# A float64 weight conversion whose integer intermediate moves from SBUF to the shared PSUM banks

## The chip, the cores and the metric

The kernel runs on one core of a Trainium2 chip. The metric is the device time of one execution in microseconds (us), the median over several runs. Lower is better.

## The reference

Three layers follow each other. Attention comes first, with a bias that depends on the distance of two positions; then a dense layer, whose two weight matrices arrive as float64; then a layer of eight experts, of which each token uses two.

```python
scores = scale * np.matmul(q, k.transpose(0, 1, 3, 2))          # 2 x 8 heads, 576 positions, 64 wide
h = np.maximum(x @ w1 + b1, 0.0); bias = h @ w2                  # x: log-distance ratio, hidden size 32
attn = softmax(scores + bias.transpose(2, 0, 1)[None])
x = (attn @ v)                                                   # 1152 tokens x 512
h = x @ w_in; x = (h * (1.0 / (1.0 + np.exp(-h)))) @ w_out       # 512 x 2048 and 2048 x 512, float64
# experts: the two largest of eight noisy logits, softmax weights, relu(x @ w1[e]) @ w2[e]
```

## The kernel before, in words

All products are made in pairs of float16 numbers: a value is split into a high part `hi` and a rest `lo`, and TensorE multiplies hi by hi, hi by lo and lo by hi.

The positions are cut into five chunks a to e (ORDER). For each chunk there are three kinds of work. `bias_wave` (L324 on) makes the bias table: in each of its 18 steps VectorE writes a mask `mk` (L337), TensorE multiplies it 16 times into a PSUM tile `pb` (L345, L346), VectorE and ScalarE read `pb` (L359, L361), and GpSimd adds the two results (L117, the helper STT). `attention` makes, for each of eight heads and each of the two batch entries, the scores (`pq`, L388), adds the bias and takes the maximum (L431), the exponential (L436), the float16 split (`pr`: ScalarE L438, GpSimd L117, VectorE L442), a transpose by DMA and the product with v. `moe1` and `moe1b` make the dense layer: 16 steps of 12 matmuls into a PSUM tile `ph` (L553 to L555), a tanh by ScalarE (L557), a product by VectorE (L558), the split, and then the second product `py` (L576 to L578).

The change sits in `conv` (L486 to L515), which turns the float64 weights into float32 bits and splits them. It runs 32 times (two matrices, two halves each, eight pieces of 128 x 512 each). One piece is loaded by a DMA of ScalarE's queue into `raw` (L496). VectorE makes float32 bits out of its two 32-bit halves in three instructions, all writing one tile `tt` of int32: L500 takes the high word and shifts it, L504 puts the sign and top exponent bit in, L505 the top bits of the low word. L504 and L505 read `raw` and `tt` and write `tt` in place. ScalarE scales `tt` by 32 in place (L509) and writes `hi` (L510); GpSimd subtracts (L511) and writes `lo`. All pieces take this branch (CP has every index). `tt` uses the two slots of the tag "yT" in SBUF, so a slot is held from L500 to the end of L511.

PSUM has eight banks: two tiles of two banks under the tag "pq" (scores, accumulators), one bank "av", and three banks under the tag "gen", handed out by `gen()` (L147). `pb` of the bias waves, `ph` of the dense and the expert layer and a few smaller tiles take turns in these three. A bank goes to the next tile when every reader of the last one is done.

The order of the work is set in two places. `merge` (L672 on) interleaves the pieces of work in program order by PLAN, a hand-written table of a start and a step for each: here "ci" and "co" (the conversion), "aa" to "ad" (attention), "ba" to "be" (bias waves), "ma" to "md" and "na" (dense layer). The framework's scheduler then fixes one order of instructions for each engine from that priority and from a model of the times and of free slots, and puts in the semaphore waits. An engine runs its instructions in that order, so an instruction that waits holds up all behind it on the same engine.

Of the kernel before, what the change touches and what calls it, by code (L numbers as in the profile page):

```python
# [9 lines left out]
F32 = mybir.dt.float32  # L10
F16 = mybir.dt.float16
I32 = mybir.dt.int32
U32 = mybir.dt.uint32
AF = mybir.ActivationFunctionType
# [94 lines left out]
def body(ctx, tc, nc, A):  # L109
    out = A["out"]  # L110
    V, SC, G, PE, SP = nc.vector, nc.scalar, nc.gpsimd, nc.tensor, nc.sync
    mm = PE.matmul

    def STT(eng, o, x, scale, y, op=OP.subtract):

        if eng is G and scale == 1.0:
            G.tensor_tensor(o, x, y, op=op)  # L117
        else:
            V.scalar_tensor_tensor(o, x, scale, y, op0=OP.mult, op1=op)
# [6 lines left out]
    def follow(later, key):  # L126
        if key in LAST:
            after(later, LAST[key])
# [11 lines left out]
    ps = ctx.enter_context(tc.tile_pool(name="ps", bufs=1, space=PSUM))  # L140
    s_m1 = ExitStack()
    m1 = s_m1.enter_context(tc.tile_pool(name="m1", bufs=1, side="right"))
# [175 lines left out]
    def wtile():  # L318
        i = used[0] % 8
        used[0] += 1  # L320
        return WB[:, 4096 * i:4096 * i + 4096]
# [164 lines left out]
    def conv(key, half, src):  # L486

        hi, lo = wtile(), wtile()
        WT[key, half] = (hi, lo)
        for pc in range(8):  # L490
            if pc % 3 in RG.get((key, half), ()):
                raw = m1.tile([128, 512], mybir.dt.int64, name="raw", tag="gt", bufs=NGT)
            else:
                raw = m1.tile([128, 512], mybir.dt.int64, name="raw", tag="raw", bufs=NRAW)
            with tc.issue_after(LAST[GATE].ins):
                SC.dma_start(raw, src(pc))  # L496
            v = raw.bitcast(I32).rearrange("p (n t) -> p n t", t=2)
            lw, hw = v[:, :, 0], v[:, :, 1]
            tt = m1.tile([128, 512], I32, name="tt", tag="yT", bufs=2)
            i = V.tensor_scalar(tt, hw, 0x07FFFFFF, 3, op0=OP.bitwise_and, op1=OP.logical_shift_left)  # L500
            if (key, half) in GC:
                follow(i, GC[key, half])
            LAST["tt", key, half, pc] = i
            V.scalar_tensor_tensor(tt, hw, -1073741824, tt, op0=OP.bitwise_and, op1=OP.bitwise_or)  # L504
            V.scalar_tensor_tensor(tt, lw, 29, tt, op0=OP.logical_shift_right, op1=OP.bitwise_or)  # L505
            f = tt.bitcast(F32)
            cs = slice(512 * pc, 512 * pc + 512)
            if pc in CP[key][half]:
                SC.activation(f, f, AF.Copy, scale=32.0)  # L509
                SC.activation(hi[:, cs], f, AF.Copy)  # L510
                G.tensor_sub(lo[:, cs], f, hi[:, cs])  # L511
            else:
                SC.activation(hi[:, cs], f, AF.Copy, scale=32.0)
                STT(V, lo[:, cs], f, 32.0, hi[:, cs])
            yield  # L515

    def conv_in(half):
        w = A["w_in"].rearrange("(j p) f -> p j f", p=128)
        return conv("in", half, lambda pc: w[:, pc // 2, 1024 * half + 512 * (pc % 2):1024 * half + 512 * (pc % 2) + 512])

    def conv_out(half):
        w = A["w_out"].rearrange("(j p) d -> p j d", p=128)
        return conv("out", half, lambda pc: w[:, 8 * half + pc, :])
# [610 lines left out]
```

## Time and profile before

| what | us |
|---|---|
| median of 3 runs | 755.66 |
| lowest and highest of them | 752.59 and 762.42 |
| the profiled execution, its time | 758.37 |
| its span, first to last instruction | 756.6 |

The profile shows one execution. Engines are PE (TensorE), PEld (its weight loads), DVE (VectorE), ACT (ScalarE), POOL (GpSimd) and SP (the queue of most DMAs). A line such as L500 is a line of the kernel; L117 is the helper by which several places let GpSimd add or subtract. The duration of an instruction includes time in which it has started and cannot go on, so its shortest and its mean duration may differ.

### The profile page before, as it was taken

How to read it: one execution, taken by the hardware profiler on the slowest of the kernel's cores; microseconds unless marked ns; L12 is line 12 of the kernel's file. 1: busy time of each engine (PE TensorE's matmuls, PEld its weight loads, DVE VectorE, ACT ScalarE, POOL GpSimd, SP SyncE). 2: the span in 40 equal slices, each digit the busy share in tenths (PEclk: the TensorE clock that was granted, in tenths of full speed). 3: DMA queues.
4: the chain of work that ended last, by engine and by line, in shares of the span. 5: the costliest groups of instructions: out<-in, count | busy, mean ns of one | idle time of the engine just before them, and what ended most of it. 6: DMA issues, size and time to landing. Idle time of an engine off the chain costs nothing.

```text
span 756.6 us, 16562 instructions
## 1 busy us (share of the span) xinstructions
PE 606.9 (80%) x6371; PEld 402.6 (53%) x6371; DVE 502.3 (66%) x1093; ACT 377.9 (50%) x805; POOL 366.5 (48%) x366
## 2 busy tenths in 40 slices
PE   0565666578587878997999889979889899999992
PEld 0462344456344666565765664757665554655640
DVE  2999999999999699556952755656657642740200
ACT  2666467668644577345732644761355543541210
POOL 2686677687967687436761552303405114103022
PEclk9875557599788998998999999999999999999996
DMA  4547788778876699887996967764999959903123
GB/s 113 135 140 243 158 161 179 183 210 186 159 179 182 161 174 199 145 172 116 159 237 124 183 129 220 192 225 110 238 240 246 308 182 230 299 4 42 17 25 43
DMA packets 203143, 125.77 MB, mean 166 GB/s; under 512 B 153076, under 2 KB 175732, under 8 KB 203060
## 3 DMA queue, kind: packets, MB, share of 16 engines
q1 hardware_dynamic: 170868, 90.39, 52.2%
q10 hardware_dynamic: 27648, 24.32, 11.0%
q0 software_dynamic: 4544, 9.97, 7.1%
q8 instruction: 51, 0.84, 0.4%
q14 instruction: 32, 0.26, 0.1%
HBM read 74.83 MB, written 18.22 MB: 123 GB/s over the span
## 4 chain that ended last, share of the span: by engine, by line
PE 29%; DVE 29%; DMA 18%; issue 11%; ACT 4%; POOL 4%; SPq 3%; ACTq 1%; another core or an unknown queue 1%; DVEq 0%; POOLq 0%
DMA stg<-in_e 6%; DVE mk L337 4%; PE ph L979 3%; DVE z L431 3%; DMA pt<-pr 3%; PE ph L981 3%; DVE pr L442 3%; PE ph L980 3%; DVE tt L504 3%; DVE tt L505 3%; PE po L1010 3%; DVE tt L500 2%; PE po L996 2%; PE po L995 2%; PE po L997 2%
## 5 line engine op out<-in xcount | busy, mean ns | idle before, releaser
L117 POOL TENSOR_TENSOR pr<-z,pr 128x512 f16<-128x512 f32 x72 | 94.6, 1321 | 23.3 <-ACT pr L438 14.7
L553 PE MATMUL ph<-xT,wb 128*128 128x256 f16 (+1 forms) x320 | 84.9, 275 | 11.5 <-DVE th L558 7.1
L345 PE MATMUL pb<-rhs_h,mk 128*128 128x64 f16 (+1 forms) x720 | 66.4, 210 | 26.4 <-ACT ta L361 11.6
L337 DVE TENSOR_TENSOR mk<-io,tau 128x1024 f16<-128x1024 f16 (+1 forms) x90 | 85.8, 959 | 0.7 <-PE pb L346 0.7
L117 POOL TENSOR_TENSOR gt<-th,gt 128x256 f16<-128x256 f32 (+1 forms) x80 | 56.0, 704 | 60.6 <-ACT gt L562 58.1
L117 POOL TENSOR_TENSOR g<-ta 128x256 f32<-128x256 f32 (+1 forms) x72 | 63.6, 884 | 44.3 <-ACT ta L361 37.4
L554 PE MATMUL ph<-xT,wb 128*128 128x256 f16 (+1 forms) x320 | 84.8, 275 | 0.0
L555 PE MATMUL ph<-xT,wb 128*128 128x256 f16 (+1 forms) x320 | 84.8, 275 | 0.0
L958 POOL DMA_INDIRECT out<-ot,idx x18 | 27.6, 1536 | 114.5 <-ACT ot L964 52.5
L388 PE MATMUL pq<-km,qt 128*128 128x512 f16 (+2 forms) x160 | 51.7, 437 | 28.9 <-DVE st L431 28.4
L436 ACT ACTIVATE z<-z,st 128x576 f32<-128x576 f32 x72 | 55.3, 769 | 34.9 <-DVE st L435 34.4
L986 DVE SCALAR_TENSOR_TENSOR ht<-ph,ht 128x320 f16<-128x320 f32 (+2 forms) x80 | 32.8, 420 | 54.3 <-ACT ht L985 53.8
L345 PEld LDWEIGHTS <-mk 128*128 128x128 f16 (+1 forms) x720 | 57.8, 111 | 19.3 <-issue 7.7
L346 PEld LDWEIGHTS <-mk 128*128 128x128 f16 (+1 forms) x720 | 56.9, 112 | 20.1 <-issue 19.2
L346 PE MATMUL pb<-rhs_l,mk 128*128 128x64 f16 (+1 forms) x720 | 65.9, 209 | 0.0
L924 DVE SCALAR_TENSOR_TENSOR wb<-stg,wb 128x1024 f16<-128x1024 f32 (+1 forms) x48 | 48.3, 1042 | 23.6 <-ACT wb L923 20.2
L923 ACT ACTIVATE wb<-stg 128x1024 f16<-128x1024 f32 (+1 forms) x48 | 41.8, 908 | 33.5 <-DMA stg<-in_e 29.9
L576 PE MATMUL py<-wb,gt 128*128 128x512 f16 x144 | 56.0, 391 | 1.5 <-DVE st L431 1.3
L577 PE MATMUL py<-wb,gt 128*128 128x512 f16 x144 | 56.1, 389 | 1.1 <-POOL wb L511 1.1
L578 PE MATMUL py<-wb,gt 128*128 128x512 f16 x144 | 55.8, 388 | 0.0
L985 ACT ACTIVATE ht<-ph 128x320 f16<-128x320 f32 (+2 forms) x80 | 29.2, 378 | 50.0 <-PE ph L981 49.8
L511 POOL TENSOR_TENSOR wb<-tt,wb 128x512 f16<-128x512 f32 x32 | 43.7, 1366 | 17.3 <-ACT wb L510 17.1
(198 smaller groups left out, 1794.0 us busy)
## 6 DMA issues: line engine op xcount, KB each, us to landing
stg<-in_e SPq DMA_DIRECT2D x64, 512.0 KB
raw<-in_w_in ACTq DMA_DIRECT2D x16, 512.0 KB
raw<-in_w_out ACTq DMA_DIRECT2D x16, 512.0 KB
bt<-eb SPq DMA_DIRECT2D x24, 288.0 KB
eb<-g SPq DMA_DIRECT2D x12, 512.0 KB
yrows<-yh SPq DMA_DIRECT2D x9, 256.0 KB
out<-zero SPq DMA_DIRECT2D x3, 768.0 KB
bt<-eb SPq DMA_DIRECT2D x16, 144.0 KB
```

The costliest lines, as they stand in the source:

```text
L117: G.tensor_tensor(o, x, y, op=op)
L337: i = V.tensor_tensor(mk[:, :, :n], io16[:, None, i0:i0 + n].to_broadcast([128, 8, n]), tv, op=OP.is_gt)
L345: mm(pb[:n, :, t, :], m, rhs_h, start=True, stop=False)
L346: mm(pb[:n, :, t, :], m, rhs_l, start=False, stop=True)
L388: i = mm(pq[p0:p0 + n, :512].rearrange("p (m s) -> p m s", m=2), lt, KM[b][r0:r0 + nr, :, h].rearrange("p m x s -> p m (x s)"), start=star ...
L436: SC.activation(z, z, AF.Exp, bias=st[:, 2:3], scale=0.125, accum_out=sums[:, bi, h % 4:h % 4 + 1])
L553: mm(ph, hh[:, cs], xh, start=(j == 3), stop=False)
L554: mm(ph, hh[:, cs], xl, start=False, stop=False)
L555: mm(ph, hl[:, cs], xh, start=False, stop=(j == 0))
L576: mm(pys[i], gh, oh[:, cs], start=(f == 0), stop=False)
L577: mm(pys[i], gh, ol[:, cs], start=False, stop=False)
L578: mm(pys[i], gl, oh[:, cs], start=False, stop=(f == 15))
```

## The change

`tt` is taken from the "gen" banks of PSUM instead of the tag "yT" of SBUF. Since GpSimd works from SBUF here, ScalarE's first instruction no longer scales in place: it reads `tt` and writes a new float32 tile `fs` in SBUF, which takes the two "yT" slots, and the two instructions after it read `fs`. The number and the kind of instructions stay the same on every engine.

```diff
-            tt = m1.tile([128, 512], I32, name="tt", tag="yT", bufs=2)
+            tt = ps.tile([128, 512], I32, name="tt", tag="gen", bufs=3)
             i = V.tensor_scalar(tt, hw, 0x07FFFFFF, 3, op0=OP.bitwise_and, op1=OP.logical_shift_left)
...
             f = tt.bitcast(F32)
             cs = slice(512 * pc, 512 * pc + 512)
             if pc in CP[key][half]:
-                SC.activation(f, f, AF.Copy, scale=32.0)
-                SC.activation(hi[:, cs], f, AF.Copy)
-                G.tensor_sub(lo[:, cs], f, hi[:, cs])
+                fs = m1.tile([128, 512], F32, name="fs", tag="yT", bufs=2)
+                SC.activation(fs, f, AF.Copy, scale=32.0)
+                SC.activation(hi[:, cs], fs, AF.Copy)
+                G.tensor_sub(lo[:, cs], fs, hi[:, cs])
```

## Rows read from the trace of the kernel before

**Rows 1.** The page: busy time by engine, and VectorE's forty slices.

```profile
PE 606.9 (80%) x6371; PEld 402.6 (53%) x6371; DVE 502.3 (66%) x1093; ACT 377.9 (50%) x805; POOL 366.5 (48%) x366
...
DVE  2999999999999699556952755656657642740200
```

**Rows 2.** Busy time by stretch; last three columns: clock, DMA share, GB/s.

```profile
50.00:246.00 196.00, 130.25 (x1506) 86.34 (x1504) 194.59 (x340) 121.12 (x254) 146.70 (x125) 0.73 0.75 183
...
150.00:200.00 50.00, 37.83 (x444) 29.00 (x442) 49.11 (x100) 38.36 (x91) 41.27 (x38) 0.89 0.82 198
...
246.00:460.00 214.00, 187.62 (x2350) 133.34 (x2349) 140.59 (x387) 113.26 (x284) 123.60 (x148) 0.96 0.81 161
```

**Rows 3.** The chain that ended last, from 50 to 246 us, by line.

```profile
by line: issue 17.9%; DVE mk L337 12.4%; DVE tt L504 11.6%; DVE tt L505 9.9%; DVE tt L500 9.0%; DVE z L431 8.6%; DVE pr L442 8.0%; DVE ta L359 3.9%; DVE vl L119 2.6%; PE pq L388 2.4%; DVE sums L464 1.7%; POOL wb L511 1.6%; DVE xh L471 1.4%;
```

**Rows 4.** VectorE's groups by line from 50 to 246 us.

```profile
L337 DVE TENSOR_TENSOR mk<-io,tau 128x1024 f16<-128x1024 f16 x38 | 39.4, 1046 | 0.0
L505 DVE SCALAR_TENSOR_TENSOR tt<-raw,tt 128x512 int32<-128x512 int32 x32 | 34.8, 1086 | 0.3
L504 DVE SCALAR_TENSOR_TENSOR tt<-raw,tt 128x512 int32<-128x512 int32 x32 | 31.5, 983 | 0.3
L500 DVE TENSOR_SCALAR tt<-raw 128x512 int32<-128x512 int32 x32 | 22.8, 712 | 0.0
L442 DVE TENSOR_TENSOR pr<-z,pr 128x64 f16<-128x64 f32 x32 | 20.9, 659 | 0.0
...
L431 DVE CUSTOM_DVE_ANT_0 z<-pq,wb 128x576 f32<-128x576 f32 x16 | 11.9, 745 | 0.0
...
L558 DVE SCALAR_TENSOR_TENSOR th<-th,ph 128x256 f32<-128x256 f32 x16 | 6.4, 406 | 0.3 <-ACT th L557 0.3
```

**Rows 5.** The tile tt: shortest, median and longest duration, first and last start.

```profile
L500 DVE TENSOR_SCALAR tt<-raw x32: 409/517/1396, 52.2 to 236.8; 128x512 int32<-128x512 int32 x32
L504 DVE SCALAR_TENSOR_TENSOR tt<-raw,tt x32: 676/694/1661, 55.0 to 239.1; 128x512 int32<-128x512 int32 x32
L505 DVE SCALAR_TENSOR_TENSOR tt<-raw,tt x32: 677/1042/1652, 58.6 to 242.2; 128x512 int32<-128x512 int32 x32
L509 ACT ACTIVATE tt<-tt x32: 613/630/635, 59.9 to 242.9; 128x512 f32<-128x512 f32 x32
...
L511 POOL TENSOR_TENSOR wb<-tt,wb x32: 1144/1220/2270, 63.1 to 245.0; 128x512 f16<-128x512 f32 x32
```

**Rows 6.** Timeline around 110 us: start, duration, instruction.

```profile
109.66 1.34 POOL L117 TENSOR_TENSOR pr<-z,pr 128x512 f16<-128x512 f32 x1
...
109.91 1.64 DVE L504 SCALAR_TENSOR_TENSOR tt<-raw,tt 128x512 int32<-128x512 int32 x1
...
111.48 0.69 DVE L337 TENSOR_TENSOR mk<-io,tau 128x1024 f16<-128x1024 f16 x1
111.51 1.23 POOL L117 TENSOR_TENSOR g<-ta 128x256 f32<-128x256 f32 x1 [0.51 <-ACT ta L361]
```

**Rows 7.** Timeline: first matmul and last reader of two pb tiles.

```profile
66.29 0.24 PE L345 MATMUL pb<-rhs_h,mk 128*128 128x64 f16 x1
...
75.25 0.38 ACT L361 ACTIVATE ta<-pb 128x256 f32<-128x256 f32 x1 [0.54 <-POOL g L117]
...
126.31 0.26 PE L345 MATMUL pb<-rhs_h,mk 128*128 128x64 f16 x1
...
129.43 0.38 ACT L361 ACTIVATE ta<-pb 128x256 f32<-128x256 f32 x1
```

**Rows 8.** TensorE's waits from 50 to 246 us: us, times, longest.

```profile
PE pb L345 <- ACT ta L361: 11.4, 5, 3.4
PE ph L553 <- DVE th L558: 5.6, 4, 3.5
PE pb L345 <- ACT tab L361: 5.3, 3, 2.4
```

**Rows 9.** Instructions on tt from 150 to 200 us: VectorE, ScalarE, GpSimd.

```profile
150.00:200.00 50.00, 25.20 (x25) 10.92 (x18) 11.66 (x10) 0.89 0.82 198
```

## The prediction, made before the changed kernel was run

> **What bounds the kernel now.** I read the page first: its busy times, then its forty slices. Over the whole span VectorE is only 66% busy, less than TensorE, but its slices show that this is an average of two different halves: from the second to the fourteenth it stands at nines, later at two to seven [rows 1]. The table by stretch puts numbers to it: from 50 to 246 us, the time in which all 32 pieces of the weights are converted, VectorE is busy 194.6 of 196.0 us, TensorE 130, ScalarE 121, GpSimd 147 [rows 2]. The third view, the chain of waits cut to that stretch, agrees: its lines are nearly all VectorE's, and the three lines on tt make up 11.6 + 9.9 + 9.0 = 30% of it [rows 3]. So there one thing sets the pace, VectorE's queue, and what it is relieved of there should shorten the span.
>
> The fourth view is VectorE's groups by line in that stretch, read beside the shortest durations of the tile's own view. The three instructions on tt take 22.8 + 31.5 + 34.8 = 89.1 us, 46% of VectorE's time [rows 4]. They are not long by nature: L504 has a shortest duration of 676 ns and a mean of 983, L505 677 and 1086, L500 409 and 712 [rows 4, 5]. L442, with only 64 columns, takes 659 ns in the mean. Next to them stand instructions that hardly scatter: L431 on 576 columns means 745 ns, L558 on 256 columns 406 ns, and both read one operand from PSUM (pq, ph) [rows 4]. The slow ones have all their operands in SBUF. The timeline tells what they meet: a subtraction of GpSimd begins at 109.66 us and ends at 111.00; L504 begins at 109.91 and takes 1.64 us, until 111.55, which is its shortest duration of some 0.68 us after GpSimd has nearly let go. Right behind it the other side pays: GpSimd's 256 columns, begun at 111.51 beside the mask of L337, take 1.23 us [rows 6], where 512 columns take it 1.14 at the least [rows 5]. So VectorE and GpSimd shut each other out of SBUF, one instruction at a time, when VectorE takes all its operands from there; with an operand in PSUM it is not shut out. The excess over the shortest duration on tt's three lines is 89.1 - 32 x (0.409 + 0.676 + 0.677) = 32.7 us.
>
> **The change, part by part.** It leaves the counts alone: three instructions of VectorE, two of ScalarE, one of GpSimd for a piece, before and after.
>
> L504 and L505 keep one operand in SBUF (raw) and get the other, and their output, in PSUM. Price from the rows with one PSUM operand: L558 and L431 give (745 - 406) / 320 = 1.06 ns for a column, so 512 columns take 745 - 64 x 1.06 = 677 ns; the SBUF row's undisturbed median is 694 [rows 4, 5]. I take 685 ns. No row shows VectorE writing to PSUM, or reading and writing one bank in one instruction. Low end 0.68 us (no cost); high end twice that, 1.36 us, an estimate for a bank that takes the read and the write in turns, which would make the change a loss of (0.712 + 0.983 + 1.086 - 0.685 - 2.72) x 32 = 20 us. I keep the low end because every reader of PSUM here runs at its column rate.
>
> L500 has one input. Undisturbed in SBUF it takes 409 ns for the 512 columns that cost L504 676 [rows 5], so it runs faster than one column a step. With its output in PSUM I price it at the rate of the rows with an operand in PSUM, 685 ns; ends 409 (rate kept) and 712 (today's mean). So the undisturbed instruction gets dearer, and what is saved is the shutting out.
> The Trainium skill, page "VectorE: DVE Perf Modes", section "Why PSUM operands drop a tier", speaks against the change here: an instruction with an operand in PSUM loses the fast mode that needs two SBUF ports. No row of this kernel shows it for an output in PSUM. By that rule L500 is the 685 ns above; without it the sum would be 32 x 0.276 = 8.8 us better.
>
> Sum on VectorE: 32 x (0.712 + 0.983 + 1.086) = 89.0 us before, 32 x 3 x 0.685 = 65.8 after, 23.2 us less, with ends of 32 us less (L500 at 0.409) and 20 more.
>
> GpSimd keeps its 32 subtractions of L511, which take 1144 ns at the least and up to 2270 [rows 5], and its other work. While VectorE works on tt it can now run undisturbed, so these should come nearer to 1144. For VectorE's other SBUF lines, L337 and L442, this may go either way: GpSimd does the same work in less time, so it is met more often, but for a shorter wait. I set that to zero. L337 alone loses 38 x (1.046 - 0.69) = 13.5 us today by its mean and by its duration in the timeline [rows 4, 6]; half of that, 7 us, either way are the ends.
>
> ScalarE's L509 reads PSUM and writes fs: 630 ns today [rows 5]; ScalarE is busy 121 of 196 us [rows 2], so tens of ns on 32 instructions are hidden. The yT slots are now held from L509 to L511 instead of from L500, which only frees them.
>
> **The added wait.** tt now takes one of three gen banks. It would hold it from the start of L500 to the end of L509: first piece 59.9 + 0.6 - 52.2 = 8.3 us, last 242.9 + 0.6 - 236.8 = 6.7 [rows 5]; over the 32 pairs 5.9 us in the mean, so 189 us of bank in 196, one bank of the three. The tenants of today: a pb lives 3.5 us at the least (126.31 to 129.81) and 9.3 us where VectorE is late (66.29 to 75.63) [rows 7]. Most of that time is work done ahead: TensorE fills a bank and waits for VectorE. TensorE's largest waits at pb and ph, 11.4 + 5.6 + 5.3 = 22.3 us, end when ScalarE or VectorE has read a bank [rows 8]; that costs nothing while VectorE is the slower one. With about two banks left this work ahead shrinks. It hurts where the banks are used hardest, 150 to 200 us, in which TensorE makes the ph of the first dense chunk and is busy 37.8 of 50 us [rows 2]. There a ph has to be filled, read by ScalarE and by VectorE. I assume that nothing is won in this stretch: it holds 25.2 of the 89.1 us on tt, 28% [rows 9]. Cost: 0.28 x 23.2 = 6.5 us. If L500 has to wait for a bank it holds up all of VectorE's queue behind it: masks, which feed TensorE, and the maxima of the attention, on which the exponentials and the transposes wait. Low end of the price zero, high end in the rivals.
>
> After 246 us TensorE is busy 187.6 of 214 us at a clock of 0.96 [rows 2]; the work left there is the same and starts earlier, so the gain goes through to the end.
>
> Total: 23.2 - 6.5 = 16.7 us. On the profiled execution 758.4 - 16.7 = 741.7; its time stands 2.7 us above the median of the three runs, so against 755.7 I forecast 739.0. A measurement of this kernel tells about 2% (15 us) from no change; the forecast is just beyond it.
>
> **The rivals.**
> 1. More is won: the shutting out fades for the other lines too and the banks cost nothing: 23.2 + 7 = 30 us, 726. For it: the lines on tt are half of VectorE's SBUF work. Against: GpSimd's 147 us have to fit in a shorter stretch.
> 2. The gain is lost to the banks everywhere, not in one stretch: pb waits too, VectorE idles at L359 and L558, and of 23.2 us about 5 stay: 751. For it: the long lives of pb at 66 us. Against: VectorE is late there, not TensorE.
> 3. Slower: L500 stands at the head of VectorE's queue and waits for a bank whose last reader is ScalarE's L361, which itself stands behind an exponential that waits for VectorE. TensorE's longest sum of such waits is 11.4 us in five, 2.3 us each [rows 8]. It decides from 23.2 / 32 = 0.73 us a piece on; if half of the pieces meet 2.3 us, 16 x 2.3 = 37 us go, and the time is 755.7 + 37 - 23 = 770. The price of reading and writing one bank, above, would end near there as well. Against it: VectorE's idle time before these lines is 0.3 us today [rows 4], and the bank's reader is usually ahead of VectorE.
> 4. The lock isn't the cause, and the instructions stay as long as they are: then L500 at 685 changes nothing, and the time stays at 755. The even durations of L431 and L558 speak against it.
>
> **How the numbers follow.** Forecast 0.42 (own range 730 to 749), the first rival 0.15, the second 0.19, the third 0.17, the fourth 0.07. Faster by over 2% means below 740.6: all of the first, a little over half of the forecast's own range and a small part of the second, together 0.44. Slower by over 2%, above 770.8: half of the third and what lies beyond it, with the scheduler's new order as a risk of its own, 0.14. Within: 0.42. For 8 in 10 the range takes in the first rival's centre and reaches up short of the third's: 722 to 765.
>
> **What would show it.** Right: L504 and L505 near 0.68 us with mean and median together, L500 near 0.68, VectorE's sum on tt at 66 us, the last L511 some 15 us earlier than 245 us, GpSimd's L511 shorter in the mean. The banks: more idle time of TensorE before L345 and L553. Wrong: idle time of VectorE before L500, means of L504 above 0.9 us, or L337 and L442 longer by what tt has lost.

## The result, and the profile after

The changed kernel took 760.56 us (median of 21 runs, 755.34 to 768.48) beside 756.94 us for the kernel before on the same chip: a ratio of 1.0059 with a 95% interval of 1.0034 to 1.0085. It is slightly slower; the forecast was 739, the range 722 to 765. The profiled execution after has a span of 764.2 us, 7.6 more than before; it ran 5.4 us over its kernel's median and the one before 1.4, so some 4 of the 7.6 us belong to these two executions and not to the kernels. From the conversion on, lines of the kernel after have numbers one higher (L509 to L511 are now L510 to L512, L553 is L554, L558 is L559).

The page first: the busy times and VectorE's slices, which answer to [rows 1].

```profile
PE 613.3 (80%) x6371; PEld 408.3 (53%) x6371; DVE 466.9 (61%) x1093; ACT 378.4 (50%) x805; POOL 348.0 (46%) x366
...
DVE  3998998689487688349742755646658542740200
```

VectorE has become 35 us cheaper and GpSimd 18, and the span is longer all the same. The row of nines is broken: from the eighth slice on it has holes, down to 4 in the eleventh (191 to 210 us). The busy time by stretch (columns as in [rows 2]: stretch, length, PE, PEld, DVE, ACT, POOL, clock, DMA share, GB/s) says where:

```profile
50.00:246.00 196.00, 133.38 (x1522) 89.78 (x1522) 161.58 (x342) 122.39 (x255) 126.23 (x125) 0.72 0.84 186
...
125.00:150.00 25.00, 15.49 (x166) 11.89 (x166) 16.61 (x35) 18.53 (x35) 14.14 (x13) 0.50 0.67 190
150.00:200.00 50.00, 37.50 (x366) 25.39 (x364) 41.18 (x97) 35.49 (x81) 33.62 (x35) 0.89 1.10 211
200.00:246.00 46.00, 37.44 (x472) 25.93 (x473) 31.80 (x58) 18.60 (x42) 26.09 (x28) 0.82 0.71 142
246.00:460.00 214.00, 184.98 (x2314) 131.87 (x2312) 132.87 (x369) 108.56 (x277) 119.14 (x145) 0.94 0.73 154
```

VectorE is busy 161.6 of 196 us where it was busy 194.6. Its free 34 us went to nobody: TensorE did only 3 us more, and with TensorE busy 15.5 of 25 us from 125 to 150 us its granted clock there is 0.50, all of it at 1.2 GHz (0.64 before). The tile views of `tt` and of `fs` after answer to [rows 5]:

```profile
L500 DVE TENSOR_SCALAR tt<-raw x32: 666/683/697, 52.6 to 215.2; 128x512 int32<-128x512 int32 x32
L504 DVE SCALAR_TENSOR_TENSOR tt<-raw,tt x32: 678/684/697, 54.9 to 216.0; 128x512 int32<-128x512 int32 x32
L505 DVE SCALAR_TENSOR_TENSOR tt<-raw,tt x32: 675/685/696, 57.7 to 216.9; 128x512 int32<-128x512 int32 x32
L510 ACT ACTIVATE fs<-tt x32: 574/597/598, 58.4 to 217.7; 128x512 f32<-128x512 f32 x32
```
```profile
L512 POOL TENSOR_TENSOR wb<-fs,wb x32: 1152/1159/1708, 60.4 to 219.3; 128x512 f16<-128x512 f32 x32
```

The scatter is gone: longest and shortest are 31 ns apart where they were almost 1000. The last piece is converted at 219 us, 26 us earlier. VectorE's groups by line, 50 to 246 us, answer to [rows 4] (busy us, mean ns, idle time before and what ended it):

```profile
L337 DVE TENSOR_TENSOR mk<-io,tau 128x1024 f16<-128x1024 f16 x38 | 35.0, 926 | 1.6 <-PE pb L346 1.6
L500 DVE TENSOR_SCALAR tt<-raw 128x512 int32<-128x512 int32 x32 | 21.9, 686 | 15.4 <-DMA raw<-in_w_out 13.6 <-DMA raw<-in_w_in 0.7 <-ACT fs L510 0.7
L504 DVE SCALAR_TENSOR_TENSOR tt<-raw,tt 128x512 int32<-128x512 int32 x32 | 21.9, 686 | 0.2
L505 DVE SCALAR_TENSOR_TENSOR tt<-raw,tt 128x512 int32<-128x512 int32 x32 | 21.9, 686 | 0.2
L442 DVE TENSOR_TENSOR pr<-z,pr 128x64 f16<-128x64 f32 x32 | 17.2, 539 | 1.3 <-ACT pr L438 1.2
```

For a bank (released by L510) L500 waits 0.7 us in all. It waits 14.3 us for the loads of `raw`, which it has caught up with. So the conversion is no longer short of VectorE; it runs ahead of everything else. What does not run ahead is shown by the masks of the bias waves, VectorE's L337 alone, by stretch (stretch, length, busy and count, clock, DMA share, GB/s), before and then after:

```profile
125.00:150.00 25.00, 2.84 (x3) 0.64 0.67 174
150.00:200.00 50.00, 2.41 (x3) 0.89 0.82 198
200.00:246.00 46.00, 15.88 (x14) 0.81 0.70 169
```
```profile
125.00:150.00 25.00, 2.14 (x3) 0.50 0.67 190
150.00:200.00 50.00, 0.00 (x0) 0.89 1.10 211
200.00:246.00 46.00, 13.82 (x17) 0.82 0.71 142
```

Not one mask is made between 150 and 200 us, where there were three, though VectorE now has 9 us free there. The table of the third bias wave is made of 18 masks. Its seventh mask started at 203 us before and starts at 227 us after; its last mask ends at 244 us before and at 243 after. So the table is not ready later than before, but hardly earlier either, although VectorE has been relieved. VectorE's timeline shows why (start, duration): in its fixed order all but the first three masks of that wave stand behind the last piece of the conversion.

```profile
216.90 0.69 DVE L505 SCALAR_TENSOR_TENSOR tt<-raw,tt 128x512 int32<-128x512 int32 x1
...
220.66 0.42 DVE L359 TENSOR_TENSOR ta<-pb,xij 128x256 f32<-128x256 f32 x1 [0.31 <-PE pb L346]
221.00 0.69 DVE L337 TENSOR_TENSOR mk<-io,tau 128x1024 f16<-128x1024 f16 x1
```

Other waits of that stretch say who else uses the banks (us in total, times, longest). They answer to [rows 8].

```profile
PE av L456 <- DMA pt<-pr: 15.6, 10, 3.5
...
PE pb L345 <- ACT fs L510: 7.6, 3, 3.6
...
PE pp L448 <- ACT fs L510: 2.9, 1, 2.9
```

L510 is the reader that frees a bank from `tt`: TensorE waits for it 7.6 us with a `pb` and 2.9 us with a `pp`, the tile through which it transposes the last two heads of the first chunk. VectorE's product with `ph` is made 11 times between 150 and 200 us, where it was made all 16 times before (L559, before L558). The first line, TensorE waiting for transposes by DMA, was 1.9 us before; the share of the DMA engines from 150 to 200 us has risen from 0.82 to 1.10.

The third chunk's attention starts when its table has been loaded (`bt`), and this is where the 26 us have gone: VectorE's first L431 of that chunk, before and after.

```profile
260.37 0.76 DVE L431 CUSTOM_DVE_ANT_0 z<-pq,bt 128x576 f32<-128x576 f32 x1 [1.16 <-DMA bt<-eb]
```
```profile
256.77 0.76 DVE L431 CUSTOM_DVE_ANT_0 z<-pq,bt 128x576 f32<-128x576 f32 x1 [1.17 <-DMA bt<-eb]
```

Of 26 us, 3.6 are left there. From that point to the end of ScalarE's last output tile (`ot`) the kernel after needs more time than the kernel before, 493.5 us against 482.5; that part has its own paragraph below ("Open").

### The profile page after: what moved, and what is told of

It is laid out like the page before. It is cut to its first block, busy times and chain, and to the rows that moved or that the text cites. A ratio compares the mean times of both kernels' runs of the same rounds, so it can differ in the third digit from the quotient of the medians.

```text
span 764.2 us, 16568 instructions
## 1 busy us (share of the span) xinstructions
PE 613.3 (80%) x6371; PEld 408.3 (53%) x6371; DVE 466.9 (61%) x1093; ACT 378.4 (50%) x805; POOL 348.0 (46%) x366
## 5 line engine op out<-in xcount | busy, mean ns | idle before, releaser
L117 POOL TENSOR_TENSOR pr<-z,pr 128x512 f16<-128x512 f32 x72 | 85.1, 1187 | 48.5 <-ACT pr L438 35.9
L554 PE MATMUL ph<-xT,wb 128*128 128x256 f16 (+1 forms) x320 | 86.9, 281 | 7.2 <-DVE th L559 3.6
L555 PE MATMUL ph<-xT,wb 128*128 128x256 f16 (+1 forms) x320 | 86.9, 281 | 0.0
L556 PE MATMUL ph<-xT,wb 128*128 128x256 f16 (+1 forms) x320 | 86.6, 281 | 0.0
L117 POOL TENSOR_TENSOR gt<-th,gt 128x256 f16<-128x256 f32 (+1 forms) x80 | 53.7, 674 | 68.7 <-ACT gt L563 68.6
L337 DVE TENSOR_TENSOR mk<-io,tau 128x1024 f16<-128x1024 f16 (+1 forms) x90 | 81.4, 912 | 3.2 <-PE pb L346 3.2
L117 POOL TENSOR_TENSOR g<-ta 128x256 f32<-128x256 f32 (+1 forms) x72 | 59.0, 819 | 38.9 <-ACT ta L361 38.7
L456 PE MATMUL av<-vh,pt 128*128 128x64 f16 (+1 forms) x400 | 38.5, 206 | 30.9 <-DMA pt<-pr 29.9
L925 DVE SCALAR_TENSOR_TENSOR wb<-stg,wb 128x1024 f16<-128x1024 f32 (+1 forms) x48 | 48.3, 1043 | 21.9 <-ACT wb L924 21.8
L431 DVE CUSTOM_DVE_ANT_0 z<-pq,bt 128x576 f32<-128x576 f32 x56 | 41.5, 749 | 28.2 <-DMA bt<-eb 20.2
L577 PE MATMUL py<-wb,gt 128*128 128x512 f16 x144 | 55.1, 383 | 0.2 <-DVE th L559 0.2
L578 PE MATMUL py<-wb,gt 128*128 128x512 f16 x144 | 55.1, 383 | 0.0
```

Of the source, the lines that this page charges most:

```text
L337: i = V.tensor_tensor(mk[:, :, :n], io16[:, None, i0:i0 + n].to_broadcast([128, 8, n]), tv, op=OP.is_gt)
L554: mm(ph, hh[:, cs], xh, start=(j == 3), stop=False)
L555: mm(ph, hh[:, cs], xl, start=False, stop=False)
L556: mm(ph, hl[:, cs], xh, start=False, stop=(j == 0))
L577: mm(pys[i], gh, oh[:, cs], start=(f == 0), stop=False)
L578: mm(pys[i], gh, ol[:, cs], start=False, stop=False)
```

## The experiments

The theory: the change does for VectorE what was forecast, but a scheduler that hands out three banks gives `tt` turns which the other users of the banks need: the bias waves, `pp` and `ph`. With these put elsewhere or earlier in the order, the gain has to appear, and the same reordering has to be worth nothing with `tt` in SBUF. The rivals: the PSUM placement itself costs what it saves (then no order helps); an order that came out badly would come out badly with either placement (then the controls move alike); or VectorE, once relieved, is held by the loads of the weights (the "loads theory" of the expectations). One rival is not tested: the plan was written by hand for the old placement and may be fitted to it, so that a changed number may cost time there for that reason alone. Ratios are to the kernel before on the same chip.

**Half the pieces.** `tt` in PSUM for one of the two matrices only.

```diff
-            tt = ps.tile([128, 512], I32, name="tt", tag="gen", bufs=3)
+            far = key == "in"     # in the other run "out"
+            tt = ps.tile([128, 512], I32, name="tt", tag="gen", bufs=3) if far else m1.tile([128, 512], I32, name="tt", tag="yT", bufs=2)
...
+                fs = m1.tile([128, 512], F32, name="fs", tag="yT", bufs=2) if far else f
```

> Only the 16 pieces of w_in keep tt in the PSUM banks; those of w_out, whose conversion runs beside the first dense chunk and its ph tiles, go back to SBUF. Banks theory (tt beside ph leaves no bank for the pb of the third bias wave, so that wave is put behind the conversion and the third chunk's attention waits for it): the wave starts before the conversion ends, the w_in pieces still take 2.06 us of VectorE each, and half of the relief arrives: 741 to 750 us. Loads theory (the conversion now outruns its weight loads, and these set the pace from 125 us on): the attention of the third chunk starts as late as in the changed kernel, 756 to 762 us.

> The mirror of the run before: only the 16 pieces of w_out have tt in PSUM. Banks theory: tt and ph meet in the three banks as in the changed kernel, the third bias wave starts only after the last piece, and the time is 757 to 766 us, no gain in spite of 16 x 0.73 = 12 us less on VectorE. Loads theory: VectorE is relieved where loads are late, so nothing is won either, 754 to 760; the start of the third bias wave tells them apart.

w_in only: 754.75 us, 1.0023 (0.9986 to 1.0061). w_out only: 765.75, 1.0155 (1.0082 to 1.0227). The half converted beside the first dense chunk and the third bias wave does the harm, and perhaps more than both together (1.0034 to 1.0085; the intervals just meet). Its forecast was met; w_in only lies between its two. With w_in alone four masks are made between 150 and 200 us, with w_out alone none:

```profile
150.00:200.00 50.00, 3.46 (x4) 0.93 0.84 187
```
```profile
150.00:200.00 50.00, 0.00 (x0) 0.83 0.99 196
```

These are rows of L337 for w_in only and for w_out only. But w_in alone, whose 16 pieces are freed of the shutting out as well, gains nothing, and its third chunk's attention starts at 258 us, so this pair does not yet say where the gain goes. It does say that the waits for a bank are not the price: from 50 to 246 us TensorE waits 10.5 us for banks of `tt` with w_in only and 0.4 us with w_out only, the slower of the two.

**A bank less, without the change.** The kernel before with two gen banks.

```diff
-        return ps.tile([128, 512], F32, name=name, tag="gen", bufs=3)
+        return ps.tile([128, 512], F32, name=name, tag="gen", bufs=2)
```

> The kernel before, tt in SBUF, with two gen banks in place of three: the loss of a bank without the relief of VectorE. Banks theory: the third bias wave starts later than before, its end and the attention of the third chunk with it, 762 to 775 us. Loads theory: the loads are as they were, 754 to 760 us.

809.35 us, 1.0727 (1.0634 to 1.0821), above both forecasts. At the start of the third chunk's attention it is 5 us late (265 us); the rest of its 54 us is lost in stages in which there is no `tt` any more. So a bank is worth some us in the disputed stretch, but the run says little about a bank that is only lent until 219 us.

**The third wave due earlier, and its control.** One number of PLAN, with `tt` in PSUM and with `tt` in SBUF.

```diff
-"bc": (153.3, 0.38)
+"bc": (110, 0.38)
```

> The changed kernel with one number of the hand-written plan altered: the third bias wave comes due at 110 instead of 153.3, so that its pb tiles get banks before the later ph and tt tiles. Nothing else differs. Banks theory: the wave runs beside the conversion again, the attention of the third chunk starts 10 us or more earlier than 257 us, and the time is 740 to 752 us. Loads theory: VectorE still waits some 14 us for raw, and the time stays at 756 to 764 us.

> The control for the earlier third wave: the kernel before, tt in SBUF, with the wave due at 110 and nothing else. If the gain of that run came from the plan alone, this one is faster than before by the same 5 to 8 us (748 to 752). Banks theory (the gain is VectorE's relief, let through): VectorE is as full as before until 245 us, the wave's earlier start delays the ph steps and the conversion by as much, and the time is 753 to 764.

With `tt` in PSUM 748.96 us, 0.9938 (0.9896 to 0.9979); with `tt` in SBUF 764.31, 1.0167 (1.0097 to 1.0236). This pair tells the theories apart best. One and the same plan is a loss of 9 us with `tt` in SBUF, where VectorE is full, and, against the changed kernel, a gain of 11.6 with `tt` in PSUM, where VectorE has room. Between the two placements lie 15.3 us, close to the 16.7 forecast (2.3% by the ratios; the two were measured on different chips). The busy time from 50 to 246 us, PSUM and then SBUF:

```profile
50.00:246.00 196.00, 128.24 (x1571) 85.47 (x1570) 168.46 (x347) 125.42 (x261) 130.40 (x131) 0.79 0.81 193
```
```profile
50.00:246.00 196.00, 127.12 (x1508) 86.06 (x1508) 192.56 (x341) 119.78 (x251) 144.57 (x125) 0.72 0.80 189
```

and VectorE's groups in the SBUF control, shut out as in [rows 4]:

```profile
L505 DVE SCALAR_TENSOR_TENSOR tt<-raw,tt 128x512 int32<-128x512 int32 x32 | 35.3, 1105 | 0.3
L504 DVE SCALAR_TENSOR_TENSOR tt<-raw,tt 128x512 int32<-128x512 int32 x32 | 32.5, 1018 | 0.2
```

The seventh mask of the third wave starts at 202 us in the PSUM kernel, 25 earlier than in the kernel after, and the third chunk's attention at 252. VectorE waits 2.7 us for loads of the weights and not 14.3, against the loads theory. But the attention was expected 10 us earlier or more and comes 4 earlier, and it does not wait for its table, whose last mask is made 18 us earlier. Most of the gain comes behind that point: to the fourth chunk's attention it takes 72.7 us here and 78.3 in the kernel after. In the SBUF control, too, the third chunk's attention starts 4 us earlier than before, at 256, and the loss comes after it, 490 us to the last output tile against 482.5. So the pair shows that the order decides together with the placement; by which path it does so, the traces do not show.

**A shorter hold.** L505 writes to SBUF, so that a bank is held from L500 to L505 and not until ScalarE has read it; ScalarE scales in place, as before the change. Then the same with the wave due earlier, twice.

```diff
+            fs = m1.tile([128, 512], I32, name="fs", tag="yT", bufs=2)
...
-            V.scalar_tensor_tensor(tt, lw, 29, tt, op0=OP.logical_shift_right, op1=OP.bitwise_or)
+            V.scalar_tensor_tensor(fs, lw, 29, tt, op0=OP.logical_shift_right, op1=OP.bitwise_or)
```

> As the changed kernel, but the third instruction on tt (the low word) writes to the SBUF tile and ScalarE scales there in place, as before the change: a bank is held from the first to the third instruction of VectorE, not until ScalarE has read it. All three keep the price of 0.69 us. Banks theory: a bank is held some 4 us instead of 5.3, ph comes sooner than in the changed kernel, 750 to 759 us. If the length of the hold doesn't matter, 758 to 763 as the changed kernel.

> Both: the short hold of the bank, and the third wave due at 110. Banks theory: the gains add up at least in part, and this is the fastest so far, 738 to 748 us; the relief of VectorE is then worth half or more of the 16.7 us that the prediction gave it. If the two are one and the same gain, 747 to 751.

> The fastest version so far, once more, for its interval: 743 to 749 us by its first runs; 0.983 to 0.993 of the kernel before.

Alone: 760.43 us, 1.0122 (1.0043 to 1.02): nothing gained, as forecast for a hold whose length does not matter. With the wave due at 110: 746.02, 0.9882 (0.9836 to 0.9928), and in the second measurement 747.82, 0.9909 (0.9878 to 0.9941). So the length of the hold is not what decides. In the run with the shorter hold alone the third wave still stands behind the conversion (no mask from 150 to 200 us). The shorter hold costs nothing on VectorE: its L506, with the output in SBUF and one input in PSUM, is not shut out either.

```profile
L506 DVE SCALAR_TENSOR_TENSOR fs<-raw,tt x32: 670/675/690, 58.4 to 215.9; 128x512 int32<-128x512 int32 x32
```

**w_in only, with the wave due earlier.** The edits of the first and the fourth run together.

> Only the pieces of w_in have tt in PSUM, and the third wave is due at 110. Banks theory: half of VectorE's relief, all of it in the stretch before the first ph, and no tt beside ph: 742 to 752 us. If what the earlier wave gained was order alone, it comes out like the control, beside the kernel before.

754.57 us, 0.9986 (0.9948 to 1.0023). No gain on the kernel before, and above its forecast. But beside the same plan with all of `tt` in SBUF (1.0167, on the same chip) it is 1.8% faster: half of the pieces out of SBUF give most of the distance between the two placements, and a gain on the kernel before came only with the pieces of w_out out of SBUF too (0.9938).

**Both waves due earlier.** `"bb"` from 50.7 to 42 beside `"bc"` at 110.

> The changed kernel with the third bias wave due at 110, as in the run of the early wave, and the second due at 42 instead of 50.7. Banks theory (every user of the three banks, the pb of the second wave too, lost its turn to tt): the second wave ends before 125 us instead of 131, the first chunk's attention and ph come no later, and the time is 738 to 748 us, below the 749 of the early third wave. If only the third wave matters: 747 to 752.

751.28 us, 0.9944 (0.9889 to 0.9998), the same as with the third wave alone. The second wave's delay in the kernel after (its table's seventh mask 13 us later) costs nothing that can be seen.

**No `pp`, and its control.** The last two heads of the first chunk are transposed by DMA like the others, so no `pp` takes a gen bank there.

```diff
-PTP = 6
+PTP = 8
```

> The changed kernel, in which the last two heads of the first chunk are transposed by DMA like all others instead of by TensorE through a pp tile in a gen bank. Nothing else differs, the plan is the old one. Banks theory: in the changed kernel pp stands ready at 116 us and starts at 125; without it the first chunk's attention ends some 8 us or more before its 141 us, the first ph comes by as much earlier than 148 us, and the time is 748 to 758. If pp's late start is not a matter of banks, the DMA transposes are no faster and the time is 758 to 768.

> The control for the run without pp: the kernel before, tt in SBUF, whose last two heads of the first chunk are transposed by DMA. If leaving pp out was worth 11 us only because it freed banks beside tt, this one is not faster than before, 754 to 764 us. If the transposes by TensorE cost 11 us whatever tt does, 743 to 748.

With `tt` in PSUM 749.71 us, 0.9894 (0.9825 to 0.9964); with `tt` in SBUF 767.32, 1.0189 (1.0137 to 1.024). The second pair that comes apart: the same edit gains 10.9 us on the changed kernel and loses about 14 on the kernel before. In the kernel after `pp` started at 125 us though the `pr` that it reads had been written at 112 to 116; without it the first chunk's attention is done at 134 us and not at 141. Here no mask is made between 150 and 200 us either, so the gain is another one than that of the early wave. Nor has it come by the third chunk: its attention starts at 258.5 us, 1.7 later than in the kernel after, so all of the gain lies behind that point, and how the earlier first chunk leads to it is not shown. What limits this run up to there stands in TensorE's groups from 50 to 246 us:

```profile
L554 PE MATMUL ph<-xT,wb 128*128 128x256 f16 x64 | 20.8, 325 | 14.8 <-ACT fs L510 8.1 <-DVE th L559 6.7
L456 PE MATMUL av<-vh,pt 128*128 128x64 f16 x160 | 18.0, 218 | 22.6 <-DMA pt<-pr 22.6
```

`ph` waits 8.1 us for a bank that `tt` holds (1.2 us in the kernel after), and the product with v waits 22.6 us for transposes (15.6).

**The third wave from other banks.** Its `pb` tiles come from the score banks, the plan is that of the kernel after.

```diff
-PBQ = {}
+PBQ = {2: (0, 1, 2)}
```

> The changed kernel with the old plan, but the pb tiles of the third bias wave come out of the two double banks of the scores instead of the three shared ones. No due time is altered. Banks theory: what put the wave behind the conversion was the lack of a bank, so it now starts before the last piece is converted, at 185 to 205 us instead of 219, and the time is 745 to 757, below the 760 of the changed kernel. If the due times were the cause, the wave starts at 219 as before and the time is 758 to 766.

763.22 us, 1.0148 (1.009 to 1.0207). The wave does start earlier, its seventh mask at 197 us and not 227, with no change in its due time: it was the lack of a bank that had put it behind the conversion. No time is won: the score banks are now missed by what they are for. VectorE reads no scores (L431) from 185 to 211 us, and the first dense chunk's output is ready at 258 us and not at 235. VectorE waits only 1.9 us for loads here, so shorter waits for loads do not make the kernel faster either.

**Everything together.** All SBUF and all PSUM with the earlier waves and without `pp` (the PSUM kernel with the shorter hold), then the shorter hold with the third wave and without `pp`.

> Everything that eases the banks at once, with tt in PSUM: the short hold (the third instruction writes to SBUF), both bias waves earlier in the plan, no pp. Banks theory: the relief of 23 us reaches the end for the most part, 730 to 743 us. If the early third wave and the short hold were the whole of it: 744 to 749.

> The control for the run before: tt in SBUF as in the kernel before, with the same two waves earlier in the plan and no pp. Banks theory: VectorE is full until 245 us as before, nothing is won, 755 to 770 us; the distance to the run before is what tt in PSUM is worth once the banks' order suits it, 15 to 23 us.

> Short hold, third wave due at 110, and no pp: the three edits that won by themselves or together. Banks theory alone: the gains add, 735 to 743 us. DMA theory (once VectorE is relieved, the loads of the weights crowd into less time, and the transposes of the attention land late, so TensorE waits for them): no further gain, 744 to 752 us, with TensorE's wait for pt above 15 us between 50 and 246 us.

All three in PSUM 752.82 us, 0.9952 (0.9888 to 1.0017); the same in SBUF 758.77, 1.0045 (0.9985 to 1.0104). The gains do not add, and between the placements lie only 6 us here, which the intervals do not tell from none. Without the earlier second wave it is 744.03 (10 runs), 0.9821 (0.9779 to 0.9863): the fastest version, 16.5 us under the kernel after and ahead of both kernels. That is the forecast of the DMA theory, at its lower end (744 to 752 us, with a wait for `pt` above 15 us: it is 19.0), and not the 735 to 743 of gains that add; against the same kernel with `pp` (0.9909) a little is gained. Its stretch of the conversion, and three of TensorE's groups in it:

```profile
50.00:246.00 196.00, 136.94 (x1623) 93.58 (x1623) 171.52 (x362) 123.36 (x265) 135.30 (x136) 0.76 0.83 203
```
```profile
L345 PE MATMUL pb<-rhs_h,mk 128*128 128x64 f16 x328 | 32.5, 219 | 5.9 <-ACT ta L361 3.2 <-ACT tab L361 2.1 <-DVE fs L506 0.5
...
L554 PE MATMUL ph<-xT,wb 128*128 128x256 f16 x85 | 24.0, 283 | 11.4 <-DVE fs L506 8.6 <-DVE th L559 1.6 <-ACT ta L361 1.1
...
L456 PE MATMUL av<-vh,pt 128*128 128x64 f16 x160 | 17.9, 218 | 22.7 <-DMA pt<-pr 19.0 <-DVE st L435 2.5 <-ACT xT L477 1.1
```

TensorE gets 101 matmuls more done in these 196 us than in the kernel after, and the third chunk's attention starts at 244 us, 12 earlier. `pb` waits 0.5 us for a bank of `tt`, but `ph` 8.6: in all 9.1 us where it was 11.7 in the kernel after, so the gain is not in these waits.

## Why the prediction was right and wrong

**Right: the bound and the shutting out.** VectorE was full from 50 to 246 us, and its instructions on `tt` were long because GpSimd shut them out. In PSUM they take 686 ns in the mean, the forecast was 685; their sum is 3 x 21.9 = 65.7 us against 65.8. That the rival "the lock isn't the cause" is wrong is shown by the same rows, in every run with all of `tt` in PSUM. L500 is slower than its best in SBUF, 683 ns against 409, as its term said. By the Trainium skill, page "VectorE: DVE Perf Modes", section "Why PSUM operands drop a tier", this is the lost fast mode; the trace agrees.

**Mis-sized: the other lines, on the good side.** They were set to zero with 7 us either way. L337 went from 39.4 to 35.0 us and L442 from 20.9 to 17.2, 8.1 us together; GpSimd's L512 from a mean of 1366 ns to 1222. Its `pr` subtraction gained too. GpSimd meets VectorE less often, and a wait that goes may go on both sides; the runs do not separate that.

**Wrong: "the gain goes through to the end".** This is the step that failed, together with "I assume that nothing is won in this stretch … 6.5 us". The gain was to pass from VectorE to everything behind it, and the banks were to cost a part of it in one stretch of 50 us. What the traces showed: the 23 us went into one thread of the work, the conversion, which was done 26 us earlier; of that 3.6 us are left at the third chunk's attention, and none at the fourth's, which starts 2.5 us later than before. Other threads came later in the fixed order: the third wave's seventh mask by 24 us, `ph`'s last product in the first dense chunk by 22 us (198 to 220). For the third wave the cause is the lack of a bank, as the run with other banks shows. That the order, and not the placement by itself, cost the gain is shown by the early wave, which gets 11.6 us back with `tt` still in PSUM, while its control loses. The prediction judged the banks by the waits that an engine sees in the old order, and took the loss as a share of the relief in one stretch. L500 waits 0.7 us for a bank and TensorE 11.7 us for banks of `tt` (7.6 + 2.9 + 1.2 at `ph`), so as waits they look cheap. The cost was in the new order, where it shows as idle time of VectorE: 34 us, of which it stands 14.3 before pieces whose loads are not there, with its next masks behind them, and the rest in smaller waits. Idle time before L500 was one of the prediction's own signs of being wrong; it came (15.4 us), but for the loads, for which the prediction has no term. "The scheduler's new order" stood in its chances, not in its sum.

**The rivals.** The second, the gain lost to the banks everywhere, is the nearest in kind, with 9.6 us more lost than it allowed. The third named the wrong place: half of the pieces were to hold up VectorE's queue 2.3 us each for a bank, and one piece did, for 0.7 us. Reading and writing one bank in one instruction has no price either.

**What the change is worth.** The same table at two places says that it depends on the order: 4 us lost with the old plan, 15.3 us gained with the third wave due at 110, 17.6 us without `pp` (767.32 and 749.71; these two were measured beside different runs of the kernel before, by the ratios it is 3%), 6 us, not clear of noise, with all three edits (the PSUM kernel there with the shorter hold). In two of four orders that is about the forecast's 16.7 us, but more than half of it is the loss of the SBUF kernel in an order that was not made for it, so these pairs do not show that the relief itself is worth 16.7 us. Between the best order found for each placement, on one chip, lie 9.5 us (744.03 and 753.54); more orders were tried for PSUM.

**Open.** From the third chunk's attention to the last output tile the kernel after needs 493.5 us, the kernel before 482.5, and the other runs 479 to 491 (the kernel with two banks 526). More than half of the 11 us is lost before the fourth chunk's attention, whose first L431 is, before and after:

```profile
332.50 0.76 DVE L431 CUSTOM_DVE_ANT_0 z<-pq,bt 128x576 f32<-128x576 f32 x1 [2.42 <-DMA bt<-eb]
```
```profile
335.04 0.76 DVE L431 CUSTOM_DVE_ANT_0 z<-pq,bt 128x576 f32<-128x576 f32 x1 [3.68 <-DMA bt<-eb]
```

TensorE's clock was 0.83 from 380 to 400 us, where it was 1.00 before, and from 257 to 460 us TensorE waits 5.9 us instead of 1.8 for a `pb` bank that VectorE's L559 frees. No run separated that, so the 11 us by which this part is longer are not explained; some 4 of them can belong to the profiled executions. The order of the work there is another one too, though no `tt` is left. Most of what the early wave gained, and all that the run without `pp` gained, lies in this part as well. Open is also whether the transposes by DMA are the next limit: TensorE waits 13 to 25 us for them in the kernels with all of `tt` in PSUM, but it waited 20.6 us in the SBUF kernel without `pp` as well, which makes more of them, and 10.6 in the SBUF kernel with the early wave, and no run took that load away.

## What to carry to other kernels

When a tile moves out of the busiest engine's way into a pool that others share, ask first who loses turns in that pool and what starts late through it; waits seen in the old order do not price this, because the order itself will change. A freed engine is worth only what the order lets it do next, so change the plan together with the placement, and run the same plan with the old placement as control: here one number of the plan made the kernel 1.7% slower with the old placement and 0.6% faster with the new one.

## What the runs showed that had not been expected

VectorE's in-place operation on a PSUM bank (read and write by one instruction, the other operand in SBUF) runs at the rate of an undisturbed one in SBUF: 684 ns against a shortest duration of 676 for 512 columns of int32. ScalarE reads 512 columns of float32 from PSUM in 597 ns where it took 630 from SBUF [rows 5]. And the same transposes by DMA became a wait for TensorE: 15.6 us from 50 to 246 us where it had 1.9, at a DMA share of 1.10 from 150 to 200 us (0.82 before).
